# Attention into a routed two-layer MoE: a sum moved to the scalar engine, a copy moved ahead of an exponential, and the first loads and routing group regrouped

## The chip, the cores and the metric

The kernel runs on one core of one Trainium2 chip. The metric is the device time of one execution in microseconds (us), lower is better. Engines are named as in the profile: PE is TensorE (matmuls and transposes), PEld its weight loads, ACT is ScalarE, DVE is VectorE, POOL is GpSimd, SP is the sync engine, which here only issues DMAs. Each engine works through its own instructions in program order; order between engines is kept by semaphores.

## What is computed

The reference, cut to what matters. Attention is local: a row attends only within its chunk of 64.

```python
q_c, k_c, v_c = (a.reshape(8, 8, 9, 64, 64) for a in (q, k, v))      # B, H, chunks, 64, D
scores = np.matmul(q_c, k_c.transpose(0, 1, 2, 4, 3)) / np.sqrt(64)
scores = scores - np.max(scores, axis=-1, keepdims=True)
attn = np.exp(scores)
attn = attn / (np.sum(attn, axis=-1, keepdims=True) + 1e-09)
x = np.matmul(attn, v_c)  # then as 4608 tokens of 512
noisy = x @ w_gate + np.log1p(np.exp(x @ w_noise)) * noise            # 8 experts
# the two best experts of a token get weights top2_w = softmax of their two logits
out[token] = sum(top2_w[k] * (np.maximum(x[token] @ w1[e_k], 0) @ w2[e_k]) for k in (0, 1))
```

## The kernel before, in words

The 4608 tokens are 36 tiles of 128. The program has two stages.

**Attention and routing** is a software pipeline written out by hand: `attend(it)` (L672) is one turn, `it` from 0 to 39, and in it each engine gets work of several tiles. In turn `it` PE is given, in this order, the scores of tile it+1 (`scores`, L405, 16 recorded matmuls), probabilities times v of tile it-2 (`pv`, L433), on every fourth turn the router's matmul of the last four tiles (`gate_mm`, L463, line 465), the transposes of the probabilities of tile it-1 (`p_trans`, L423) and of the attention output of tile it-3 (`x_trans`, L450), and on the turn behind a gate turn the sums of the router's output (`gate_sum`, L475). DVE gets of tile `it` the row maxima (`soft_max`, L413) and their subtraction (`soft_sub`, L418), then of tile it-2 the norm in three steps: row sum plus 1e-9 (`norm_a`, L442), its reciprocal (`norm_b`, L445), and the product that evicts the attention output (`norm_c`, L448). ACT gets the exponential of tile `it` (`soft_exp`, L421), the copy of the transposed probabilities of tile it-1 out of PSUM (`p_copy`, L429), the copy of the transposed output of tile it-3 (`x_copy`, L459) and, in gate turns, one more copy (L469).

What matters for the steps below is what is single and what is double. Scores alternate between two PSUM banks. The result of `pv` has one place, banks 3 and 4 (`pvb`, L431): `norm_a` and `norm_c` read it, and `pv` of the next tile overwrites it. The transposed probabilities have one PSUM bank and two copies in SBUF, `mx` and `rc` have two buffers each.

**Routing** of a group of tiles (`route`, L480) is a generator of small DVE and ACT steps; a turn takes up to six DVE steps of it (`STEPS`, L673) behind `norm_c`. Groups are four tiles, the last eight (L109). When a group is routed, every tile of it is written twice to a table of slots in DRAM by an indirect DMA of POOL (`scatter`, L589; line 600). In front of each such write stands a tiny copy (L598) that makes POOL wait for the turn's `mx` or `rc`, so the writes are spread: one behind `mx`, one behind `rc`. POOL also does eight halves of the split of w1 (L89) in turns 12 to 26.

**The experts** follow: PE runs dense matmuls in three passes (`three`, L224, line 231) over tiles of tokens that are loaded back by expert. The first experts' blocks are loaded early, when the writes of a certain group are out (`EARLY`, L105).

Loads of q, k and v come per pair of tiles: `load_qk` (L321) and `load_v` (L328), on SP, into rings of three buffers. Only k of the first pair is issued by ACT (L341).

Of the kernel before, what the change touches and what calls it, by code (L numbers as in the profile page):

```python
# [8 lines left out]
FT = mybir.dt.float32  # L9
# [4 lines left out]
AF = mybir.ActivationFunctionType  # L14
OP = mybir.AluOpType
# [4 lines left out]
P = 128  # L20
NTOK = 4608
NT = NTOK // P
# [27 lines left out]
def kernel(ctx, tc, qT, kT, vh, wgn, noise, w1, w2, out, caps=CAPS):  # L50
    nc = tc.nc
    consts = ctx.enter_context(tc.tile_pool(name="consts", bufs=1))
# [49 lines left out]
    NJ = NLIST  # L102
    BN = max(sum(r for _, r in b) for bs in blocks for b in bs)
    LEAD = 7
    EARLY = {0: 3, 1: 6}  # L105


    NPE = nb
    groups = [(0, 4), (4, 4), (8, 4), (12, 4), (16, 4), (20, 4), (24, 4), (28, 8)]  # L109
    LAST = len(groups) - 1  # L110
    grp_of = {t: g for g, (t0, n) in enumerate(groups) for t in range(t0, t0 + n)}
    later_xg = []
# [5 lines left out]
    lwt = consts.tile([P, NJ, NE], FT, name="lwt")  # L118
    lid0 = {b: consts.tile([P, len(blocks[0][b])], I32, name=f"lid0{b}") for b in EARLY}
    lwt0 = {b: consts.tile([P, len(blocks[0][b])], FT, name=f"lwt0{b}") for b in EARLY}  # L120
    lim0 = {b: consts.tile([P, 1], FT, name=f"lim0{b}") for b in EARLY}
    meta0 = {b: consts.tile([P, len(blocks[0][b]), 3], FT, name=f"meta0{b}") for b in EARLY}
    XG, XH, HT, BX, BH, OB = {}, {}, {}, {}, {}, {}
# [9 lines left out]
    def rows_of(i, j):  # L133
        e = BL[i][0]
        k = j - blocks[0][i][0][0] if i in EARLY else 0
        return lid0[i][:, k:k + 1] if i in EARLY else lid[:, j, e:e + 1]

# [176 lines left out]
    loads = pk.enter_context(tc.tile_pool(name="loads", bufs=1))  # L314
    RING = 3
    KB = [loads.tile([P, 2, 2, 4, P], FT, name=f"kb{n}") for n in range(RING)]
    VB = [vs.tile([P, 2, 2, 2, 4, 65], FT, name=f"vb{n}") for n in range(RING)]
    QB = {}
    HALF = (slice(0, 64), slice(64, 128))

    def load_qk(j):  # L321
        if j < NT // 2:
            QB[j] = loads.tile([P, 2, 4, P], FT, name="qb", bufs=RING)
            for h in range(2):
                nc.sync.dma_start(QB[j][h::2], qT[HALF[h], 2 * j:2 * j + 2])
                nc.sync.dma_start(KB[j % RING][h::2, h], kT[HALF[h], 2 * j:2 * j + 2])
# [7 lines left out]
        nc.vector.memset(KB[0][:, :, a], 0.0)  # L334
    nc.gpsimd.memset(KB[1], 0.0)
    nc.vector.memset(VB[0], 0.0)
    QB[0] = loads.tile([P, 2, 4, P], FT, name="qb", bufs=RING)
    for a in range(2):
        for h in range(2):
            nc.sync.dma_start(QB[0][h::2, a], qT[HALF[h], a])  # L340
            nc.scalar.dma_start(KB[0][h::2, h, a], kT[HALF[h], a])  # L341
    nc.scalar.preload_act_table_set("natural_log_exp_and_others")
    load_v(0)
    jp = consts.tile([P, P], FT, name="jp")
# [4 lines left out]
    nc.vector.tensor_scalar(before, jp, 0.0, None, op0=OP.is_gt)  # L349
    ones = consts.tile([P, P], BF, name="ones")  # L350
    nc.vector.memset(ones, 1.0)
    spacer = consts.tile([1, 1], FT, name="spacer")
    e_row = consts.tile([P, NE], FT, name="e_row")
    nc.gpsimd.iota(e_row, pattern=[[1, NE]], base=0, channel_multiplier=0, allow_small_or_imprecise_dtypes=True)
# [24 lines left out]
    nc.gpsimd.memset(VB[1], 0.0)  # L379
    for t in (KB[2], VB[2]):  # L380
        nc.gpsimd.memset(t, 0.0)
    load_qk(1)
    load_v(1)
    wg = consts.tile([P, ND, 32], FT, name="wg")
    nc.sync.dma_start(wg, wgn)
# [9 lines left out]
    PR, PT, XS, XT, RC = {}, {}, {}, {}, {}  # L395
# [9 lines left out]
    def scores(t):  # L405
        for hp in range(4):
            for q in HALF:
                nc.tensor.matmul(PS[q, t % 2, hp * P:(hp + 1) * P], QB[t // 2][:, t % 2, hp, q],  # L408
                                 KB[t // 2 % RING][:, :, t % 2, hp, q], start=True, stop=True)
# [13 lines left out]
    def p_trans(t):  # L423
        for hp in range(4):
            nc.tensor.transpose(PS[:, 2, hp * P:(hp + 1) * P], PR[t][:, hp * P:(hp + 1) * P], ident)  # L425

    def p_copy(t):
        PT[t] = work.tile([P, 4, P], FT, name="pts", bufs=2)
        nc.scalar.activation(PT[t].rearrange("p a b -> p (a b)"), PS[:, 2, :], AF.Copy)  # L429

    pvb = PS[:, 3:5, 0:260].rearrange("p b (g n) -> p b g n", n=65)  # L431
# [7 lines left out]

    def norm_a(t):  # L440
        RC[t] = work.tile([P, 2, 4, 1], FT, name="rc", bufs=2)
        nc.vector.tensor_scalar(RC[t], pvb[:, :, :, 64:65], 1e-9, None, op0=OP.add)  # L442

    def norm_b(t):
        nc.vector.reciprocal(RC[t], RC[t])  # L445
# [34 lines left out]
    def route(g):  # L480
# [31 lines left out]
        m = gate.tile(n8, FT, name="gm")  # L512
        mi = gate.tile(n8, U32, name="gmi")
        for r in range(G):
            yield "dve"
            V.max(m[:, r], sp[:, r])
        for r in range(G):
            yield "dve"
            V.max_index(mi[:, r], m[:, r], sp[:, r])
        oh = gate.tile([P, 2, G, NE], FT, name="goh")  # L520
        for k in range(2):
# [67 lines left out]
    def scatter(n, gate=None):  # L589

        for _ in range(n):
            if not pending:
                return
            g, r, k = pending.pop(0)
            if gate is None:
                nc.gpsimd.memset(spacer, 0.0)
            else:
                nc.gpsimd.tensor_copy(spacer, gate)  # L598
            t0, G = groups[g]
            s = nc.gpsimd.indirect_dma_start(  # L600
                out=slots, out_offset=bass.IndirectOffsetOnAxis(ap=lii[:, k, t0 + r:t0 + r + 1], axis=0),
                in_=XS[(t0 + r) // 4][:, r % 4, 0:USED], in_offset=None)
            for o in scatters:
                tc.declare_no_dep(s.ins, o.ins, reason="every token has a slot of its own")
            for o in early_loads:
                tc.declare_no_dep(s.ins, o.ins, reason="slots of an early block are given before it is loaded")
            scatters.append(s)
            if (r, k) != (G - 1, 1):
                continue
            for i in EARLY:  # L610
                if g == EARLY[i]:
                    js = blocks[0][i][0][0]
                    m = len(blocks[0][i])
                    gather(i)
                    early_loads.append(nc.sync.dma_start(
                        meta0[i], by_slot[js * P:(js + m) * P, 0, CODE:USED].rearrange("(j p) c -> p j c", p=P)))
            if g == LAST:
                gather(len(EARLY))
# [18 lines left out]
    def step_route(phase, most=99):  # L637
        for r in list(routing):
            while r[1] == phase and most > 0:
                if phase == "dve":  # L640
                    most -= 1
                r[1] = next(r[0], None)
            if r[1] is None:
                routing.remove(r)
# [27 lines left out]
    def attend(it):  # L672
        STEPS = 6  # L673
        if it % 2:
            load_qk((it - 1) // 2 + 3)
        if it % 2 == 0 and it >= 4:
            load_v((it - 4) // 2 + 3)
        if it in (5, 7):
            for r in range(CLEAN + 64 * (it // 2 - 2), CLEAN + 64 * (it // 2 - 1), 16):
                nc.sync.dma_start(slots[r * NE:(r + 16) * NE, 0:USED], zero)  # L680
        if it == 7:
            nc.sync.dma_start(slots[(CLEAN + P) * NE:NLIST * P * NE, CODE:USED].rearrange("(p r) c -> p r c", p=P),
                              zero[:, 0:3 * (NLIST * P - CLEAN - P) // 16].rearrange("p (r c) -> p r c", c=3))
        if it in (9, 11, 13, 15):
            w_load(0, 1, (it - 9) // 2)
        if it == 32:
            zero_out(8)
        if it in (29, 31, 33, 35):
            w_load(0, 2, (it - 29) // 2)
        next_turn()  # L690
        if it == 0:
            scores(0)
        if it + 1 < NT:
            scores(it + 1)
        if 0 <= it - 2 < NT:
            pv(it - 2)
        gated = it - 4 >= 0 and (it - 4) % 4 == 3
        if gated:
            gate_mm((it - 4) // 4)
        if 0 <= it - 1 < NT:  # L700
            p_trans(it - 1)
        if 0 <= it - 3 < NT:
            x_trans(it - 3)
        if it - 5 >= 0 and (it - 5) % 4 == 3:
            gate_sum((it - 5) // 4)
            if grp_of[it - 5] != grp_of.get(it - 4):
                r = route(grp_of[it - 5])
                routing.append([r, next(r)])
        step_route("pe")
        if it < NT:  # L710
            mx = soft_max(it)
            soft_sub(it, mx)
            scatter(1, mx[0:1, 0, 0:1])
            soft_exp(it)
        if 0 <= it - 1 < NT:
            p_copy(it - 1)
        if 0 <= it - 3 < NT:
            x_copy(it - 3)
        if gated:
            gate_copy((it - 4) // 4)  # L720
        step_route("act")
        if 0 <= it - 2 < NT:
            norm_a(it - 2)
            norm_b(it - 2)
            scatter(1, RC[it - 2][0:1, 0, 0])
            norm_c(it - 2)
        step_route("dve", STEPS)
        if it > 32:
            zero_out(3)
        if it == NT + 2:  # L730
            scatter(2, XT[(it - 3) // 4][0:1, 0, (it - 3) % 4, 0:1])
        elif it == NT + 3:
            scatter(2, LS[(it - 4) // 4][0:1, 0, 0:1])
        if it in range(12, 28, 2):
            w_split(0, 1, *wq.pop(0), eng=nc.gpsimd)
# [241 lines left out]
```

## Time and profile before

| | us |
|---|---|
| median of three runs | 995.55 (994.05 to 995.59) |
| the profiled execution, its own time | 993.54 |
| its span, first to last instruction | 991.7 |
| busy: PE, DVE, ACT, POOL | 959.4, 463.9, 282.5, 225.8 |
| first scores matmul starts | 6.47 |
| first `pv` starts | 18.01 |
| `pv` of tile 34 starts | 143.55 |

The profile is one execution taken by the hardware profiler. In its lines `out<-in` gives the program's names, a shape is partitions x elements, `xN` counts instructions, and a bracket says how long the engine stood idle before the instruction and what ended that (`<-`). A fp32 matmul leaves two records, so `pv` of one tile shows as x16. The profiled time and the span differ by 1.8 us; the profiled execution lies 2.0 us below the median of the three runs.

### The profile page before, as it was taken

Reading aid. Unit: us, or ns where it says so; the run is one execution under the profiler, and the core shown is the slowest. Engines: PE = TensorE matmul, PEld = TensorE weight load, DVE = VectorE, ACT = ScalarE, POOL = GpSimd, SP = SyncE. Lnnn points to the kernel's source line nnn. Section 1 sums busy time; section 2 is a strip of 40 time slices with the busy share of each in tenths; the row PEclk is TensorE's granted clock in tenths of the full one; section 3 lists DMA queues with packets and bytes.
Section 4 is the critical chain, followed back from the end, with each engine's and each line's share of the span. In section 5 each row is a group of like instructions: output and inputs, shape, how many; then the busy total and the mean of one; then the engine's idle time right before and its main releaser. Section 6 shows DMA issues by size and latency. Waiting matters only on the chain.

```text
span 991.7 us, 16057 instructions
## 1 busy us (share of the span) xinstructions
PE 959.4 (97%) x5788; PEld 850.6 (86%) x5788; DVE 463.9 (47%) x1043; ACT 282.5 (28%) x595; POOL 225.8 (23%) x320
## 2 busy tenths in 40 slices
PE   6998988999999999999999999999999999999996
PEld 5886766898799888988998899889988998899885
DVE  6778774523445352544344434443344334433311
ACT  2565553222233221412231223132213221322100
POOL 3045556831100111121002101211111111111112
PEclk9999999999999999999999999999999999999999
DMA  8998899849611652166116622572264226402213
GB/s 300 317 368 285 293 376 395 268 143 149 180 33 33 154 136 37 33 142 149 35 28 136 159 48 28 112 178 44 32 154 133 44 32 154 112 12 32 33 22 44
DMA packets 97154, 132.92 MB, mean 134 GB/s; under 512 B 23440, under 2 KB 56592, under 8 KB 97072
## 3 DMA queue, kind: packets, MB, share of 16 engines
q1 hardware_dynamic: 80320, 93.02, 31.7%
q0 software_dynamic: 16432, 38.33, 19.3%
q8 instruction: 46, 0.75, 0.3%
q10 hardware_dynamic: 320, 0.52, 0.2%
q14 instruction: 36, 0.29, 0.1%
HBM read 81.69 MB, written 50.13 MB: 133 GB/s over the span
## 4 chain that ended last, share of the span: by engine, by line
PE 92%; DVE 4%; issue 2%; DMA 0%; POOL 0%; ACT 0%; another core or an unknown queue 0%; SPq 0%; DVEq 0%; POOLq 0%
PE PS L231 81%; PE PS L437 3%; PE PS L408 3%; PE PS L425 2%; PE PS L453 1%; PE PS L465 1%; PE PS L276 1%; DVE xs L448 1%; PE PS L478 1%; DMA kb<-in_kT 0%; POOL out L198 0%; DVE mx L413 0%; PE PS L214 0%; DVE pr L418 0%
## 5 line engine op out<-in xcount | busy, mean ns | idle before, releaser
L198 POOL DMA_INDIRECT out<-o,lid x77 | 119.9, 1557 | 662.0 <-DVE o L261 642.3
L231 PE MATMUL PS<-xh,w1h 128*128 128x384 f32 (+2 forms) x768 | 262.1, 341 | 4.8 <-issue 3.1
L231 PE MATMUL PS<-xl,w1h 128*128 128x384 f32 (+2 forms) x768 | 260.9, 340 | 0.2 <-DVE xl L222 0.2
L231 PE MATMUL PS<-xh,w1l 128*128 128x384 f32 (+2 forms) x768 | 260.9, 340 | 0.0
L250 ACT ACTIVATE hh<-PS 128x384 fp32r<-128x384 f32 (+2 forms) x192 | 95.2, 496 | 469.9 <-PE PS L231 421.3
L231 PE MATMUL PS<-w2h,hh 128*128 128x512 f32 x584 | 228.0, 390 | 0.0
L231 PE MATMUL PS<-w2h,hl 128*128 128x512 f32 x584 | 227.6, 390 | 0.0
L231 PE MATMUL PS<-w2l,hh 128*128 128x512 f32 x584 | 227.6, 390 | 0.0
L253 DVE SCALAR_TENSOR_TENSOR hl<-PS,hh 128x384 fp32r<-128x384 f32 (+2 forms) x192 | 108.6, 566 | 184.6 <-ACT hh L250 139.5
L261 DVE TENSOR_SCALAR o<-PS,lwt 128x512 f32<-128x512 f32 x77 | 57.7, 749 | 230.2 <-PE PS L231 222.9
L231 PEld LDWEIGHTS PS<-xh,w1h 128*128 128x128 f32 x768 | 144.5, 188 | 12.2 <-issue 8.2
L231 PEld LDWEIGHTS PS<-xl,w1h 128*128 128x128 f32 x768 | 144.6, 188 | 2.1 <-DVE xl L222 0.5
L231 PEld LDWEIGHTS PS<-xh,w1l 128*128 128x128 f32 x768 | 144.6, 188 | 1.0
L231 PEld LDWEIGHTS PS<-w2h,hl 128*128 128x128 f32 x584 | 109.2, 187 | 23.5
L231 PEld LDWEIGHTS PS<-w2h,hh 128*128 128x128 f32 x584 | 109.2, 187 | 22.5
L231 PEld LDWEIGHTS PS<-w2l,hh 128*128 128x128 f32 x584 | 109.2, 187 | 22.5
L600 POOL DMA_INDIRECT slots<-xs,lii x72 | 72.5, 1007 | 18.5 <-issue 17.9
L221 ACT ACTIVATE xh<-y 128x512 fp32r<-128x512 f32 x67 | 41.2, 614 | 92.6 <-DVE y L218 90.6
L222 DVE TENSOR_TENSOR xl<-y,xh 128x512 fp32r<-128x512 f32 x67 | 44.9, 671 | 48.2 <-ACT xh L221 45.4
L408 PE MATMUL PS<-kb,qb 128*64 128x128 f32 x576 | 43.2, 295 | 10.9 <-DMA kb<-in_kT 9.6
L408 PEld LDWEIGHTS PS<-kb,qb 128*64 128x64 f32 x576 | 34.0, 146 | 16.0 <-issue 13.0
L437 PE MATMUL PS<-vb,pts 128*64 128x130 f32 x576 | 40.2, 280 | 6.6 <-DVE gsm L543 1.7
(128 smaller groups left out, 701.2 us busy)
## 6 DMA issues: line engine op xcount, KB each, us to landing
st<-in_w SPq DMA_DIRECT2D x36, 512.0 KB
xg<-slots SPq DMA_DIRECT2D x252, 64.0 KB
st<-in_w SPq DMA_DIRECT2D x112, 128.0 KB
out<-zero SPq DMA_DIRECT2D x37, 256.0 KB
vb<-in_vh SPq DMA_DIRECT2D x36, 260.0 KB
qb<-in_qT SPq DMA_DIRECT2D x34, 256.0 KB
kb<-in_kT SPq DMA_DIRECT2D x34, 256.0 KB
xg<-slots SPq DMA_DIRECT2D x9, 256.0 KB
```

Of the source, the lines that this page charges most:

```text
L198: s = nc.gpsimd.indirect_dma_start(out=out, out_offset=bass.IndirectOffsetOnAxis(ap=rows_of(i, j)[0:r], axis=0), in_=o[0:r], in_offset=Non ...
L221: nc.scalar.activation(oh, src, AF.Copy)
L222: nc.vector.tensor_sub(ol, src, oh.bitcast(FT))
L231: nc.tensor.matmul(p, a, b, start=first and n == 0, stop=last and n == 2)
L250: nc.scalar.activation(hh[:, 0:n], p, AF.Relu)
L253: nc.vector.scalar_tensor_tensor(hl[:, 0:n], p, 0.0, hh[:, 0:n].bitcast(FT), op0=OP.max, op1=OP.subtract)
L261: nc.vector.tensor_scalar(o[0:r], p[0:r], w, None, op0=OP.mult)
L276: nc.tensor.matmul(p[q * r:q * r + r], HR[0][:, f, 0:r], staged[e, 2, f // 2][:, (f % 2) * DM:(f % 2) * DM + DM], start=n == 0, stop=n == ...
L408: nc.tensor.matmul(PS[q, t % 2, hp * P:(hp + 1) * P], QB[t // 2][:, t % 2, hp, q], KB[t // 2 % RING][:, :, t % 2, hp, q], start=True, stop ...
L425: nc.tensor.transpose(PS[:, 2, hp * P:(hp + 1) * P], PR[t][:, hp * P:(hp + 1) * P], ident)
L437: nc.tensor.matmul(PS[q, 3 + hp // 2, o:o + 130], PT[t][:, hp, q], VB[t // 2 % RING][:, :, t % 2, c, hp, :], start=True, stop=True)
L600: s = nc.gpsimd.indirect_dma_start(out=slots, out_offset=bass.IndirectOffsetOnAxis(ap=lii[:, k, t0 + r:t0 + r + 1], axis=0), in_=XS[(t0 + ...
```

## The change

Six edits, all in the attention stage.

1. q and k of the second pair of tiles are loaded right behind those of the first; k of it by ACT, ahead of the load of the activation table.
2. In turns 0 and 1 the PE order is other: scores of tiles 0 and 1, transposes of tile 0, scores of tile 2, then on as before.
3. On ACT, `p_copy(it-1)` stands ahead of `soft_exp(it)`; it stood behind it.
4. `norm_a` is an ACT activation (identity with a bias tile of 1e-9), placed behind `soft_exp(it)`, instead of a DVE operation.
5. The first routing group is tiles 0 to 7 in place of two groups of four, and `EARLY` is counted anew to name the same tiles. Two `max` or two `max_index` make one routing step, where one did.
6. In a turn two row writes stand behind `mx` in place of one, so a turn has up to three.

```diff
-    EARLY = {0: 3, 1: 6}
+    EARLY = {0: 2, 1: 5}
-    groups = [(0, 4), (4, 4), (8, 4), (12, 4), (16, 4), (20, 4), (24, 4), (28, 8)]
+    groups = [(0, 8), (8, 4), (12, 4), (16, 4), (20, 4), (24, 4), (28, 8)]
...
             nc.scalar.dma_start(KB[0][h::2, h, a], kT[HALF[h], a])
+    for h in range(2):
+        nc.sync.dma_start(QB[1][h::2], qT[HALF[h], 2:4])
+        nc.scalar.dma_start(KB[1][h::2, h], kT[HALF[h], 2:4])
     nc.scalar.preload_act_table_set("natural_log_exp_and_others")
     load_v(0)
...
-    load_qk(1)
     load_v(1)
...
     def norm_a(t):
         RC[t] = work.tile([P, 2, 4, 1], FT, name="rc", bufs=2)
-        nc.vector.tensor_scalar(RC[t], pvb[:, :, :, 64:65], 1e-9, None, op0=OP.add)
+        nc.scalar.activation(RC[t], pvb[:, :, :, 64:65], AF.Identity, bias=eps)
...
         for r in range(G):
-            yield "dve"
+            if r % 2 == 0:
+                yield "dve"
             V.max(m[:, r], sp[:, r])
...
         if it == 0:
             scores(0)
-        if it + 1 < NT:
+        if it <= 1:
+            p_trans(0) if it else scores(1)
+        if 0 < it < NT - 1:
             scores(it + 1)
...
+        if 0 <= it - 1 < NT:
+            p_copy(it - 1)
         if it < NT:
             mx = soft_max(it)
             soft_sub(it, mx)
-            scatter(1, mx[0:1, 0, 0:1])
+            scatter(2, mx[0:1, 0, 0:1])
             soft_exp(it)
-        if 0 <= it - 1 < NT:
-            p_copy(it - 1)
+        if 0 <= it - 2 < NT:
+            norm_a(it - 2)
         if 0 <= it - 3 < NT:
             x_copy(it - 3)
...
         if 0 <= it - 2 < NT:
-            norm_a(it - 2)
             norm_b(it - 2)
```

What ACT's program holds in turns 6 and 7, before: `pr` is the exponential, `pts` the copy of the transposed probabilities, `xt` the copy of the transposed output, `ls` the gate turn's extra copy (the numbers are those of the buffers).

```order
L421 ACTIVATE pr_416<-pr_416 128x512
L429 ACTIVATE pts_419<-PS_72 128x512
L459 ACTIVATE xt_299<-PS_72 128x4x128
L421 ACTIVATE pr_467<-pr_467 128x512
L429 ACTIVATE pts_470<-PS_72 128x512
L459 ACTIVATE xt_472<-PS_72 128x4x128
L469 ACTIVATE ls_474<-PS_72 128x512
```

And the same two turns now, where `rc` is the moved `norm_a`:

```order
L434 ACTIVATE pts_416<-PS_72 128x512
L426 ACTIVATE pr_420<-pr_420 128x512
L447 ACTIVATE rc_423<-PS_72,eps_143 128x8
L464 ACTIVATE xt_303<-PS_72 128x4x128
L434 ACTIVATE pts_467<-PS_72 128x512
L426 ACTIVATE pr_471<-pr_471 128x512
L447 ACTIVATE rc_474<-PS_72,eps_143 128x8
L464 ACTIVATE xt_476<-PS_72 128x4x128
L474 ACTIVATE ls_478<-PS_72 128x512
```

The copy and the exponential have changed places, and `rc` stands third, behind both.

On DVE, a plain turn and the head of the next before: maxima, subtraction, then the three steps of the norm.

```order
L413 TENSOR_REDUCE mx_331<-PS_72 128x8
L418 TENSOR_TENSOR pr_333<-PS_72,mx_331 128x4x2x64
L442 TENSOR_SCALAR rc_339<-PS_72 128x8
L445 RECIPROCAL rc_339<-rc_339 128x8
L448 TENSOR_TENSOR xs_261<-PS_72,rc_339 128x512
L413 TENSOR_REDUCE mx_376<-PS_72 128x8
```

Now:

```order
L418 TENSOR_REDUCE mx_335<-PS_72 128x8
L423 TENSOR_TENSOR pr_337<-PS_72,mx_335 128x4x2x64
L450 RECIPROCAL rc_340<-rc_340 128x8
L453 TENSOR_TENSOR xs_263<-PS_72,rc_340 128x512
L418 TENSOR_REDUCE mx_380<-PS_72 128x8
```

One instruction a turn is gone from DVE, and the reciprocal now reads what ACT has written.

At the start PE's program was this (`kb_108`, `kb_109` and `kb_110` are k of the first, second and third pair of tiles, `vb` is v):

```order
L408 MATMUL PS<-kb_108,qb 64x128 x16
L408 MATMUL PS<-kb_109,qb 64x128 x8
L425 MATMUL PS<-ident,pr 128x128 x4
L408 MATMUL PS<-kb_109,qb 64x128 x8
L437 MATMUL PS<-vb_111,pts 64x130 x8
```

and is now this:

```order
L413 MATMUL PS<-kb_108,qb 64x128 x16
L430 MATMUL PS<-ident,pr 128x128 x4
L413 MATMUL PS<-kb_109,qb 64x128 x16
L442 MATMUL PS<-vb_111,pts 64x130 x8
L430 MATMUL PS<-ident,pr 128x128 x4
```

The transposes of tile 0 stand ahead of the scores of tile 2.

More of the change, by code (lines that the diff above doesn't have):

```diff
@@ L336 @@
     nc.vector.memset(VB[0], 0.0)
-    QB[0] = loads.tile([P, 2, 4, P], FT, name="qb", bufs=RING)
+    for j in range(2):
+        QB[j] = loads.tile([P, 2, 4, P], FT, name="qb", bufs=RING)
     for a in range(2):
@@ L351 @@
     nc.vector.memset(ones, 1.0)
+    eps = consts.tile([P, 1], FT, name="eps")
+    nc.vector.memset(eps, 1e-9)
     spacer = consts.tile([1, 1], FT, name="spacer")
@@ L514, in route @@
         for r in range(G):
-            yield "dve"
+            if r % 2 == 0:
+                yield "dve"
             V.max(m[:, r], sp[:, r])
         for r in range(G):
-            yield "dve"
+            if r % 2 == 0:
+                yield "dve"
             V.max_index(mi[:, r], m[:, r], sp[:, r])
@@ L699, in attend @@
             gate_mm((it - 4) // 4)
-        if 0 <= it - 1 < NT:
+        if 0 < it - 1 < NT:
             p_trans(it - 1)
@@ L712, in attend @@
             soft_sub(it, mx)
-            scatter(1, mx[0:1, 0, 0:1])
+            scatter(2, mx[0:1, 0, 0:1])
             soft_exp(it)
-        if 0 <= it - 1 < NT:
-            p_copy(it - 1)
+        if 0 <= it - 2 < NT:
+            norm_a(it - 2)
         if 0 <= it - 3 < NT:
```

## The prediction

> **What bounds the kernel now.** I read the page, then the busy time by stretches, then the timeline of one turn.
>
> ```profile
> PE 959.4 (97%) x5788; PEld 850.6 (86%) x5788; DVE 463.9 (47%) x1043; ACT 282.5 (28%) x595; POOL 225.8 (23%) x320
> ```
> ```profile
> 18.00:36.00 18.00, 18.00 (x242) 15.11 (x240) 13.98 (x30) 8.83 (x16) 0.00 (x0) 1.00 0.95 338
> 112.00:128.00 16.00, 14.92 (x189) 12.18 (x186) 12.63 (x52) 8.49 (x20) 10.02 (x19) 1.00 0.91 309
> 148.00:174.00 26.00, 20.49 (x130) 17.40 (x130) 13.04 (x65) 8.71 (x21) 15.87 (x27) 0.93 1.04 395
> 174.00:230.00 56.00, 55.63 (x283) 48.79 (x284) 21.94 (x70) 11.04 (x22) 31.41 (x50) 1.00 0.68 188
> ```
>
> A stretch gives its length, then the busy time of PE, PEld, DVE, ACT and POOL, the granted clock, DMA share and GB/s. From 174 us on PE is busy 55.63 of 56: the experts are a block of matmuls, and whatever delays their start delays the end one for one. So the change is priced in the attention stage alone. There PE is full in plain turns (18.00 of 18.00) and nearly so with routing (14.92 of 16).
>
> One plain turn, from one `pv` to the next, in the timeline (start, duration):
>
> ```profile
> 26.59 1.06 PE L437 MATMUL PS<-vb,pts 128*64 128x130 f32 x16
> 27.58 0.65 PE L425 MATMUL PS<-ident,pr 128*128 128x128 f32 x4
> 27.70 0.17 DVE L442 TENSOR_SCALAR rc<-PS 128x8 f32<-128x8 f32 x1 [0.41 <-PE PS L437]
> 27.90 0.20 DVE L445 RECIPROCAL rc<-rc 128x8 f32<-128x8 f32 x1
> 28.14 0.69 DVE L448 TENSOR_TENSOR xs<-PS,rc 128x512 f32<-128x512 f32 x1
> 28.34 0.60 ACT L429 ACTIVATE pts<-PS 128x512 f32<-128x512 f32 x1 [0.38 <-PE PS L425]
> 28.83 0.59 ACT L459 ACTIVATE xt<-PS 128x512 f32<-128x512 f32 x1
> 29.53 1.06 PE L437 MATMUL PS<-vb,pts 128*64 128x130 f32 x16
> ```
>
> See that the norm starts 0.05 us after `pv` ends (26.59 + 1.06 = 27.65, then 27.70) and its eviction is over at 28.83, 0.70 before the next `pv` at 29.53 overwrites the banks. That slack is why PE sets the turn: 2.94 us.
>
> **The change: the norm moves onto a ring.** ACT runs in order. `norm_a(t)` now stands behind the exponential of tile t+2, that behind `p_copy(t+1)`, that waits for `p_trans(t+1)`, and that stands on PE behind `pv(t)`. And `pv(t+1)` may not start before `norm_c(t)` has read the banks. So from `pv` to `pv` runs one closed chain. Its links that the plain turn doesn't show, from waits of the same kind:
>
> ```profile
> 120.18 0.63 ACT L421 ACTIVATE pr<-pr 128x512 f32<-128x512 f32 x1 [1.34 <-DVE pr L418]
> 120.72 0.58 ACT L429 ACTIVATE pts<-PS 128x512 f32<-128x512 f32 x1
> 121.35 1.11 PE L437 MATMUL PS<-vb,pts 128*64 128x130 f32 x16
> 122.39 0.66 PE L425 MATMUL PS<-ident,pr 128*128 128x128 f32 x4
> ```
> ```profile
> 109.12 0.69 DVE L448 TENSOR_TENSOR xs<-PS,rc 128x512 f32<-128x512 f32 x1 [0.20 <-DVE rc L445]
> 109.95 1.11 PE L437 MATMUL PS<-vb,pts 128*64 128x130 f32 x16 [1.07 <-DVE xs L448]
> ```
> ```profile
> 149.12 0.60 ACT L221 ACTIVATE xh<-PS 128x512 fp32r<-128x512 f32 x1 [0.98 <-PE PS L214]
> 149.75 0.69 DVE L222 TENSOR_TENSOR xl<-PS,xh 128x512 fp32r<-128x512 f32 x1 [0.78 <-ACT xh L221]
> ```
> ```profile
> L496 ACT ACTIVATE gy<-PS 128x32 f32<-128x32 f32 x7 | 1.4, 200 | 1.7 <-PE PS L478 1.5 <-PE PS L535 0.2
> ```
>
> `pv` to `p_trans` 1.04 (121.35 to 122.39, a `pv` that had waited); `p_trans` to `p_copy` 0.76 (27.58 to 28.34); `p_copy` to the next on ACT 0.49 (28.34 to 28.83); exponential to the next 0.54 (120.18 to 120.72); `norm_a`, which no row shows on ACT, 0.21 (nearest: 200 ns for 32 columns out of PSUM, plus a little for the bias); ACT's end to DVE 0.03 (149.72 to 149.75); reciprocal to `norm_c` 0.24; `norm_c` 0.69; its end to `pv` 0.14 (109.81 to 109.95). Sum 4.14; I take **4.1 us a turn**, with 3.95 (`pv` not slowed by the wait, DVE to PE at nothing) and 4.3 as ends. PE's other work of the turn, `x_trans` and scores, fits beside it.
>
> The Trainium skill gives another price for `norm_a`: ScalarE: Activation LUTs, What ACT_TABLE_LOAD costs, has an activation whose bias is a pointer operand at about 280 ns plus 0.833 ns a column, so 0.29 by estimate. By that page the ring is 4.22 and the change 2.7 us dearer over the stage; no row here has this exact form, and the nearest is shorter.
>
> How many turns, and what they took:
>
> ```profile
> 18.01 1.28 PE L437 MATMUL PS<-vb,pts 128*64 128x130 f32 x16
> 143.55 1.11 PE L437 MATMUL PS<-vb,pts 128*64 128x130 f32 x16 [0.31 <-issue]
> L437 PE MATMUL PS<-vb,pts 128*64 128x130 f32 x544 | 37.8, 279 | 6.6 <-DVE gsm L543 1.7 <-ACT xt L459 1.2 <-ACT pr L421 1.2
> 33.45 1.06 PE L465 MATMUL PS<-xt,wg 128*32 128x512 f32 x8
> 34.45 0.66 PE L425 MATMUL PS<-ident,pr 128*128 128x128 f32 x4
> ```
>
> The group counts the window from 20 us: 544 / 16 = 34 `pv` behind the first, so 34 intervals took 143.55 - 18.01 = 125.5 us. All 34 go over the ring (the last exponential is in turn 35). In 8 of them the router's matmul lies between `pv` and `p_trans`: 1.00 more each (33.45 to 34.45). 34 x 4.1 + 8 x 1.0 = 147.4.
>
> **Routing steps** stand on DVE between `norm_c` and the next maxima:
>
> ```profile
> 71.10 0.18 DVE L503 SCALAR_TENSOR_TENSOR gu<-gu,gy 128x32 f32<-128x32 f32 x1
> 72.18 0.68 DVE L413 TENSOR_REDUCE mx<-PS 128x8 f32<-128x512 f32 x1
> ```
>
> Five opening steps take 1.08 (71.10 to 72.18). With steps R, maxima and subtraction (0.72 each: the 0.68 of the maxima taken for both, and a gap) end R + 1.34 after `pv`, while ACT gets to the exponential at 2.29 (1.04 + 0.76 + 0.49); so R up to 0.95 is hidden, and 1.95 in a gate turn. A full turn of six steps is some 1.2, and pairing two `max` a step fills more turns; about ten turns without a gate exceed by 0.25: +2.5 (0 to 5). What edits 4 and 5 take off DVE, 0.2 a turn and the steps of one group, is worth nothing while the ring ends later than DVE: 147.4 + 2.5 - 125.5 = **+24.4 us**. `p_copy` ahead of the exponential frees `pv` from a late subtraction, which shortens nothing while `pv` waits for `norm_c`.
>
> **The start.**
>
> ```profile
> 6.47 3.68 PE L408 MATMUL PS<-kb,qb 128*64 128x128 f32 x32 [6.47 <-DMA kb<-in_kT]
> 8.28 0.59 SPq L326 DMA_DIRECT2D kb<-in_kT  x1
> 9.93 0.63 ACT L421 ACTIVATE pr<-pr 128x512 f32<-128x512 f32 x1 [4.15 <-DVE pr L418]
> 13.29 1.98 PE L408 MATMUL PS<-kb,qb 128*64 128x128 f32 x16 [3.14 <-DMA kb<-in_kT]
> 15.20 1.12 PE L425 MATMUL PS<-ident,pr 128*128 128x128 f32 x4
> ```
>
> The scores of tile 2 wait 3.14 us for k, issued last at 8.28. Now it is issued ahead of v and should be there when the transposes of tile 0 are done: exponential over at 10.56, transposes 1.12, so about 11.7. Two tiles of scores at half of 3.68 each: `pv` at 15.4, or earlier as the clock rises, against 18.01: **-3.0** (-1 if the first k lands later for sharing, to -4).
>
> **Else.** POOL's writes come every 1.35 us:
>
> ```profile
> 89.33 1.01 POOL L600 DMA_INDIRECT slots<-xs,lii  x1 [0.16 <-issue]
> 90.68 0.99 POOL L600 DMA_INDIRECT slots<-xs,lii  x1 [0.16 <-issue]
> ```
>
> Three are 4.05, within a turn; only the first group's 16 beside three w1 halves run up to 2 us behind, which two buffers of `mx` and `rc` take up: 0 (0 to 2). DVE also waited for PE beyond what its program needs:
>
> ```profile
> DVE rc L442 <- remote: 3.7, 2, 2.1
> DVE rc L442 <- PE PS L453: 3.4, 2, 1.8
> ```
>
> The cause isn't shown. These 7.1 us lie in the 125.5; on the ring they may come on top: 0 to 7, I take +1.5. Behind the stage PE idles 5.5 of 26 us (148 to 174) while DMA is full (1.04); a longer stage leaves transfers less crowded: -1.5 (-4 to 0).
>
> Sum: 24.4 - 3.0 + 1.5 - 1.5 = +21.4. The profiled execution took 993.54, so 1014.9 on its scale; it lies 2.0 below the median of 995.55, on which I put the forecast: 1017, rounded down to **1016**.
>
> **Rivals.** *DVE is the bound and the ring is hidden* (faster). Where routing runs, DVE is busy 12.63 of 16, and DVE's waits for PE are few; if `norm_a` came in time, 34 x 0.2 = 6.8 from the moved sum (27.70 to 27.90), some 3 from a group's steps (five took 1.08; a group has about 20, and the double group's wider ones give part back) and 3.0 at the start: 995.5 - 12.8 = 983. It decides if the chain falls under the old mean of 125.5 / 34 = 3.69 a turn; `p_trans`, `p_copy` and exponential alone put `norm_a` at 2.83 of it, against the change. Chance 0.06.
>
> *The clock falls* (slower still). The ring leaves PE idle about 1 us in 4.
>
> ```profile
> 74.00:78.00 4.00, 2.26 (x28) 2.04 (x26) 2.65 (x9) 1.86 (x4) 2.39 (x4) 0.81 0.95 337
> 105.00:112.00 7.00, 5.44 (x67) 3.63 (x62) 4.52 (x16) 2.53 (x6) 4.84 (x9) 1.00 0.91 287
> ```
>
> With PE busy 2.26 of 4 the granted clock fell to 0.81; with 5.44 of 7 (78%) it stayed 1.00, and the ring is at 3.1 of 4.1 (76%). If a third of the 150 us ran at half clock, PE's two links (1.80) would double in 12 turns: +21.6, so 1038. Chance 0.07. The Trainium skill (TensorE: Matmul & The Clock Gate, Why this matters for your kernels) asks for gaps above about 3 us before the clock drops; by that rule this rival has no chance. The trace disagrees: at 74 the clock fell with 4.00 - 2.26 = 1.74 us idle in all.
>
> *The ring costs half* (slower, less): the waits for PE and the crowded stretch behind go, and routing turns, dearer than the mean of 3.69 before, lose little: 996 to 1004. Chance 0.08, a quarter of it within 0.2%.
>
> That the change does not do what it says is excluded by the order of instructions.
>
> **How the numbers follow.** Forecast 0.79. The range takes the ring at 3.95 (-5.1), no routing excess (-2.5), no recurring waits (-1.5) and the start and the stretch behind a little better (1004), and the ring at 4.3 (+6.8) with the waits at +7 (1028). A measurement here tells about 0.2%, 2 us. Faster 0.06, same 0.02, slower 0.92.
>
> **What would show it.** Right: plain turns of 4.1 us, with `norm_c` releasing `pv` in nearly every turn and the reciprocal waiting for ACT; first `pv` near 15. Wrong: plain turns still near 2.9, or `pv` released by PE's own order.

## The result and the profile after

| | before | after |
|---|---|---|
| median, us | 995.57 (994.05 to 997.12) | 1039.13 (1036.69 to 1040.5) |
| ratio, 95% interval | | 1.0435 (1.0409 to 1.0461) |
| the profiled execution, its own time and span | 993.54, 991.7 | 1036.69, 1034.7 |
| first `pv`, `pv` of tile 34 | 18.01, 143.55 | 14.27, 187.08 |

The change made the kernel slower, as forecast, but by 43.6 us, not 20.5: 1039.13 lies above the range of 1004 to 1028. The kernels below ran on several chips of the same kind; the kernel before took 981 to 982 us on two of them and 995 to 999 on the others, so every kernel is compared with the kernel before on its own chip, by ratio.

First the page's busy line and the stretches of after: the attention stage up to tile 18, the rest of it, and the experts.

```profile
PE 971.5 (94%) x5787; PEld 856.2 (83%) x5787; DVE 457.0 (44%) x993; ACT 284.9 (28%) x625; POOL 226.4 (22%) x320
```
```profile
14.20:94.70 80.50, 62.99 (x787) 50.07 (x782) 45.02 (x121) 37.44 (x90) 6.90 (x8) 1.00 0.78 260
94.70:187.00 92.30, 66.10 (x692) 51.63 (x692) 49.88 (x188) 36.35 (x96) 49.92 (x81) 0.87 0.83 295
...
217.00:300.00 83.00, 82.49 (x402) 72.52 (x403) 32.41 (x84) 19.83 (x39) 30.44 (x49) 0.98 0.66 157
```

PE is busy 62.99 of 80.50 us (78%) in the first half of the stage, where before it was full in plain turns. In the second half the granted clock is 0.87. Behind 217 us the experts run as before.

The start and the end of the stage, on PE:

```profile
14.27 1.07 PE L442 MATMUL PS<-vb,pts 128*64 128x130 f32 x16
...
17.95 1.09 PE L413 MATMUL PS<-kb,qb 128*64 128x128 f32 x16 [2.02 <-DMA kb<-in_kT]
...
187.08 1.21 PE L442 MATMUL PS<-vb,pts 128*64 128x130 f32 x10 [2.06 <-ACT ls L474]
```

The stage from `pv` of tile 0 to that of tile 34 takes 187.08 - 14.27 = 172.8 us, 47.3 more than the 125.5 before. The start gives back 3.7, and behind tile 34 the span has 1034.7 - 187.08 = 847.6 us left against 848.2. So the whole miss lies between tiles 0 and 34.

One plain turn of after, all engines, with DVE's and ACT's other rows left out:

```profile
63.00 1.11 PE L442 MATMUL PS<-vb,pts 128*64 128x130 f32 x16 [0.23 <-ACT gu L503]
...
64.03 0.66 PE L430 MATMUL PS<-ident,pr 128*128 128x128 f32 x4
...
64.73 0.60 ACT L434 ACTIVATE pts<-PS 128x512 f32<-128x512 f32 x1 [0.76 <-PE PS L430]
...
65.22 0.62 ACT L426 ACTIVATE pr<-pr 128x512 f32<-128x512 f32 x1
65.74 0.26 ACT L447 ACTIVATE rc<-PS,eps 128x8 f32<-128x8 f32 x1
...
66.03 0.20 DVE L450 RECIPROCAL rc<-rc 128x8 f32<-128x8 f32 x1 [1.86 <-ACT rc L447]
...
66.34 0.69 DVE L453 TENSOR_TENSOR xs<-PS,rc 128x512 f32<-128x512 f32 x1
...
67.14 1.11 PE L442 MATMUL PS<-vb,pts 128*64 128x130 f32 x16 [0.98 <-ACT xt L464]
```

This is the forecast ring, link by link: 1.03, 0.70, 0.49, 0.52, 0.29, 0.31, 0.69 and 0.11, in sum 4.14 us. PE's last wait is put down to ACT's `xt`, but `norm_c` ends at 67.03, 0.11 ahead of `pv`; that is the one it needs. Two links were longer than forecast, `norm_a` to reciprocal at 0.29 (0.24) and reciprocal to `norm_c` at 0.31 (0.24); the others were shorter by as much.

The second half is different. The turn from tile 18 to tile 19 takes 6.65 us instead of 4.2:

```profile
94.73 1.11 PE L442 MATMUL PS<-vb,pts 128*64 128x130 f32 x16 [1.04 <-issue]
...
95.76 0.99 POOL L607 DMA_INDIRECT slots<-xs,lii  x1 [0.16 <-issue]
...
95.77 0.66 PE L430 MATMUL PS<-ident,pr 128*128 128x128 f32 x4
...
97.32 0.98 POOL L607 DMA_INDIRECT slots<-xs,lii  x1 [0.40 <-issue]
...
98.64 0.98 POOL L607 DMA_INDIRECT slots<-xs,lii  x1 [0.16 <-issue]
...
98.93 0.60 ACT L434 ACTIVATE pts<-PS 128x512 f32<-128x512 f32 x1 [4.35 <-PE PS L483]
...
101.38 1.52 PE L442 MATMUL PS<-vb,pts 128*64 128x130 f32 x16 [2.69 <-ACT gu L503]
```

By PE's rows the transposes end at 95.77 + 0.66 = 96.43. ACT is free and waits for them, and its copy starts only at 98.93: 2.50 us late, where a plain turn has 0.04. I call this a late signal of PE. POOL's row writes stand back to back around it, five from 92.90 to 98.64. Three more such turns:

```profile
126.84 0.66 PE L430 MATMUL PS<-ident,pr 128*128 128x128 f32 x4
...
130.53 0.60 ACT L434 ACTIVATE pts<-PS 128x512 f32<-128x512 f32 x1 [5.29 <-remote]
...
145.13 0.66 PE L430 MATMUL PS<-ident,pr 128*128 128x128 f32 x4
...
149.43 0.60 ACT L434 ACTIVATE pts<-PS 128x512 f32<-128x512 f32 x1 [5.04 <-remote]
...
168.16 0.66 PE L430 MATMUL PS<-ident,pr 128*128 128x128 f32 x4
...
172.03 0.60 ACT L434 ACTIVATE pts<-PS 128x512 f32<-128x512 f32 x1 [4.61 <-remote]
```

"remote" means that no instruction in the trace ends where the wait does. The four are 2.50, 3.03, 3.64 and 3.21 us late, 12.4 in sum, and on the ring nothing hides them. Since the ends of matmuls are modelled, the rows don't tell whether PE's work or only its signal came late; the times of the semaphore updates, which the trace holds but no view prints, do. In the plain turn above PE's signals come 0.01 to 0.02 us behind the ends of its rows. In the last of the three turns here `pv` and the two sets of transposes end at 168.23, 168.82 and 169.26 by the rows, and their signals come at 171.94, 172.00 and 172.06, only 0.06 us apart, where the rows end 0.43 us and more apart. So the work was done, and its signals were held up.

POOL's rows up to 190 us hold just four runs of five writes with under 1.75 us from start to start, from 92.90, 123.89, 142.20 and 164.80 on, and each has one of the four late signals at its end. Beside the six runs of two or three ACT's copy never waits over 1 us for its signal; by the semaphore updates a signal of `pv` or of the scores is 1.1 to 1.9 us late behind each of the four runs of three, but the ring doesn't wait for that one. The length of a run isn't all: in the second trace of after (experiment 6) a run of six from 104.54 on brought no more than 1.1 us.

### The profile page after: what moved, and what is told of

It is laid out like the page before. It is cut to its first block, busy times and chain, and to the rows that moved or that the text cites. A ratio compares the mean times of both kernels' runs of the same rounds, so it can differ in the third digit from the quotient of the medians.

```text
span 1034.7 us, 16013 instructions
## 1 busy us (share of the span) xinstructions
PE 971.5 (94%) x5787; PEld 856.2 (83%) x5787; DVE 457.0 (44%) x993; ACT 284.9 (28%) x625; POOL 226.4 (22%) x320
## 4 chain that ended last, share of the span: by engine, by line
PE 83%; DMA 6%; ACT 3%; DVE 2%; issue 2%; POOL 1%; SPq 1%; another core or an unknown queue 0%; DVEq 0%; ACTq 0%; POOLq 0%
PE PS L231 77%; PE PS L442 2%; DMA kb<-in_kT 1%; PE PS L430 1%; DMA vb<-in_vh 1%; DMA out<-zero 1%; ACT pr L426 1%; PE PS L276 1%; DMA st<-in_w 1%; ACT pts L434 1%; DMA slots<-xs,lii 1%; PE PS L470 1%; DVE xs L453 1%; DMA slots<-zero 1%
## 5 line engine op out<-in xcount | busy, mean ns | idle before, releaser
L442 PE MATMUL PS<-vb,pts 128*64 128x130 f32 x576 | 44.5, 299 | 39.6 <-ACT ls L474 8.4
L442 PEld LDWEIGHTS PS<-vb,pts 128*64 128x64 f32 x576 | 35.9, 147 | 47.0 <-ACT ls L474 9.9
```

The source lines that it names most:

```text
L442: nc.tensor.matmul(PS[q, 3 + hp // 2, o:o + 130], PT[t][:, hp, q], VB[t // 2 % RING][:, :, t % 2, c, hp, :], start=True, stop=True)
```

## The experiments

Two theories at first. **R**: the ring alone lays late signals open, whatever the writes do. **W**: the third row write (edit 6) makes them. A third, **X**, came up with the first traces: the output rows. The rows of four tiles share one of five buffers, which comes free when their eight writes have landed, and the group of eight (edit 5) starts the writes later. A fourth, **C**, came up with the chips: the late signals belong to the chip and come with any writes.

**1. The ring alone.** The kernel before with edits 3 and 4:

```diff
+        if 0 <= it - 1 < NT:
+            p_copy(it - 1)
...
             soft_exp(it)
-        if 0 <= it - 1 < NT:
-            p_copy(it - 1)
+        if 0 <= it - 2 < NT:
+            norm_a(it - 2)
```

> The kernel before with edits 3 and 4 alone (copy ahead of the exponential, norm_a on ACT behind it): the ring, without the new start, the group of eight and the third row write. Theory W (the late turns are long because PE's results are signalled 2.5 to 3.6 us late where five or more row writes follow each other 1.3 us apart): with two writes a turn the runs of writes are short, plain turns of 4.2 us from first to last, 1017 to 1025. Theory R (the ring alone lays the late signals open, however the writes are grouped, and the clock falls for it): as after less the start's gain, 1038 to 1046.

Measured: 1017.11 us against 982.04, ratio 1.0358 (1.0327 to 1.0388). The turns are 4.1 to 4.3 us from first to last, with no late signal. The time is what W expected, but the kernel before was 13 us faster on this chip than on the first, so the ratio fitted neither and the question had to be put again on other chips.

**2. After without the ring.** `norm_a` back on DVE, everything else as in after:

```diff
-        nc.scalar.activation(RC[t], pvb[:, :, :, 64:65], AF.Identity, bias=eps)
+        nc.vector.tensor_scalar(RC[t], pvb[:, :, :, 64:65], 1e-9, None, op0=OP.add)
...
-        if 0 <= it - 2 < NT:
-            norm_a(it - 2)
...
         if 0 <= it - 2 < NT:
+            norm_a(it - 2)
             norm_b(it - 2)
```

> The kernel after with norm_a back on DVE at its old place; everything else stays. Both theories: no ring, plain turns of 2.9 to 3.2 us. Theory W: the third write still bunches the writes, late signals of 2 us and more stay and cost 3 to 8 us, 994 to 1002. Theory R: only the start's gain of 3.7 us and what DVE saves are left, 985 to 993.

Measured: 995.37 against 982.04, ratio 1.0128 (1.0096 to 1.0161). So edits 5 and 6 cost something without the ring too, as W said, but on this chip not by late signals (none): `norm_c` of tile 20 waited 5.3 us for row writes, the clue to X.

**3. After with two writes a turn.**

```diff
-            scatter(2, mx[0:1, 0, 0:1])
+            scatter(1, mx[0:1, 0, 0:1])
```

> The kernel after with one row write behind the maxima instead of two, so two a turn. Theory W: the four late signals of 2.5 to 3.6 us go or fall under 1.5 us, the clock keeps to 1.00 up to tile 30, 1015 to 1026. Theory R: they stay, 1035 to 1043.

Measured: 1045.11 against 982.04, ratio 1.0657 (1.0621 to 1.0694): neither. Taking the third write out of after made it worse (after itself was at 1.0435 on the first chip). DVE in the turn of tile 20:

```profile
111.79 0.69 DVE L453 TENSOR_TENSOR xs<-PS,rc 128x512 f32<-128x512 f32 x1 [4.96 <-DMA slots<-xs,lii]
```

`norm_c` writes into the buffer of tiles 0 to 3 and waits until the last of its eight writes has landed. Two writes a turn are eight in four turns, just what four tiles bring, so a late start is never made up: such a wait came at tiles 20, 24, 28 and 32 (turns of 8.2 to 9.2 us). So with edit 5 in place the third write also has its use: with it `norm_c` hardly waits (experiments 5 to 8).

**4. The new start alone.** Edits 1 and 2 on the kernel before.

```diff
+    for h in range(2):
+        nc.sync.dma_start(QB[1][h::2], qT[HALF[h], 2:4])
+        nc.scalar.dma_start(KB[1][h::2, h], kT[HALF[h], 2:4])
...
+        if it <= 1:
+            p_trans(0) if it else scores(1)
```

> The kernel before with edits 1 and 2 alone (second pair's q and k loaded first, order of turns 0 and 1). If the start's gain reaches the end: first pv near 14.3 instead of 18.0 and 992 (-3.7). Rival: the later turns wait for their loads or for the slots and give it back: 994 to 997.

Measured: ratio 1.000 (0.9985 to 1.0015). PE at the start of this kernel, and the third `pv` of the kernel before (on the first chip):

```profile
13.85 1.05 PE L440 MATMUL PS<-vb,pts 128*64 128x130 f32 x16
...
18.13 1.09 PE L411 MATMUL PS<-kb,qb 128*64 128x128 f32 x16 [2.64 <-DMA kb<-in_kT]
...
23.61 1.05 PE L440 MATMUL PS<-vb,pts 128*64 128x130 f32 x16
```
```profile
23.66 1.06 PE L437 MATMUL PS<-vb,pts 128*64 128x130 f32 x16
```

The first `pv` comes 4 us earlier, then the scores of a later tile wait for the next k, and by the third `pv` the gain is gone (23.61 against 23.66). The load was not moved out of the way, only the wait for it moved. With the ring part of the gain stays (experiment 9).

**5 to 8. Which chip, which edit.** On another chip, with the kernel before run for its profile, the kernel after again, after with edit 5 undone, and before with edit 5 alone:

```diff
-    groups = [(0, 8), (8, 4), (12, 4), (16, 4), (20, 4), (24, 4), (28, 8)]
+    groups = [(0, 4), (4, 4), (8, 4), (12, 4), (16, 4), (20, 4), (24, 4), (28, 8)]
```

(with `EARLY` and the routing steps as before; edit 5 alone is the same lines the other way round, on the kernel before)

> The kernel before, unchanged, for its profile on the chip of this call. If this chip is like the one of the first experiments: about 982, plain turns of 2.9 us and none of the late signals of PE that stood between 66 and 145 us; if like the first chip, 994 to 996.

> The kernel after, unchanged, beside its parts on the same chip. Theory X (the ring, plus a ring of buffers: the output rows of four tiles hold a buffer of five until their eight writes have landed; the group of eight starts the writes some four turns later, so from tile 20 on norm_c waits for them): ratio to before 1.045 to 1.06, with waits of norm_c for row writes of 3 to 6 us at every fourth tile. Theory R (the ring, plus late signals of PE as on the first chip): ratio 1.036 or less if this chip shows no late signals.

> The kernel after with edit 5 undone: groups of four, one max a step, the early blocks as before. Theory X: no wait of norm_c for row writes, plain turns of 4.2 us to the end, ratio 1.030 to 1.038, that of the ring alone. Theory R: as the kernel after beside it, within 0.5%.

> The kernel before with edit 5 alone: the first group of eight, steps in pairs, early blocks renumbered. Theory X: two writes a turn of 2.9 us start some four turns later and never catch up, so norm_c waits for them from tile 20 on, once per four tiles: 5 to 20 us slower, ratio 1.005 to 1.02. Theory R: 0 to 3 us, ratio 0.997 to 1.003.

Measured: before 995.32, with late signals; after 1.0459 (1.0409 to 1.0510), with late signals of 2.5 to 4.1 us in the same four turns as in its first trace; after with groups of four 1.0450 (1.0404 to 1.0496); before with the group of eight 1.0283 (1.0234 to 1.0332). So X falls for after, though the ratio is the one it forecast: undoing edit 5 changes nothing there, and `norm_c` hardly waits for row writes. By itself, though, with two writes a turn, edit 5 costs 27 us, more than X expected. The waits of `norm_c` in the first trace of after (14 to 190 us), with ACT's waits that end at nothing, and in before with edit 5 (20 to 170 us); the columns are total, times, longest:

```profile
ACT pts L434 <- remote: 14.9, 3, 5.3
...
DVE xs L453 <- DMA slots<-xs,lii: 0.8, 3, 0.3
```
```profile
DVE xs L448 <- DMA slots<-xs,lii: 26.3, 4, 7.2
```

**9. Ring and start, without edits 5 and 6**, on one of the 981 us chips:

> The kernel after with edits 5 and 6 undone: groups of four and two row writes a turn, so the ring and the new start alone. Theory W (three writes a turn make PE's results late where five follow each other): plain turns of 4.2 us throughout, no late signal over 1 us, ratio 1.031 to 1.038. Theory C (the late signals belong to the chip and come with any writes): on a chip like the first, late signals of 2 to 4 us stay and the ratio is 1.041 to 1.050; on a chip without them 1.031 to 1.038.

Measured: ratio 1.0314 (1.0290 to 1.0339), no late signal, as both theories allow on such a chip. It is 0.4% under the ring alone (1.0358 on another chip of that kind), but the intervals overlap, so the ratios don't show that the start's gain is kept. The traces do in part: the first `pv` comes at 13.80 against 17.61 with the ring alone, the third at 23.66 against 25.95, so 2.3 of the 3.8 us are left by then.

**10. The third write alone**, edit 6 on the kernel before, same chip.

> The kernel before with edit 6 alone, three row writes a turn. My recorded step has it at nothing (0 to 2 us): ratio 0.998 to 1.003. Theory W: late signals of 2 to 4 us where five writes follow each other, half of it hidden by the slack of plain turns: ratio 1.005 to 1.015. Theory C: as the kernel before, 0.998 to 1.003.

Measured: ratio 1.0061 (1.0042 to 1.0080). The ratio is the one W forecast, but not for W's reason. ACT's copy starts over 1 us behind the transposes twice, by 2.2 and 1.2 us, and both times ACT was held by its exponential, which waited for DVE's subtraction:

```profile
72.15 0.66 PE L425 MATMUL PS<-ident,pr 128*128 128x128 f32 x4
...
74.44 0.63 ACT L421 ACTIVATE pr<-pr 128x512 f32<-128x512 f32 x1 [3.45 <-DVE pr L418]
74.97 0.58 ACT L429 ACTIVATE pts<-PS 128x512 f32<-128x512 f32 x1
```

By the semaphore updates no signal of PE is over 1 us late in this trace, although POOL's writes stand in runs of up to eight there. My step had the third write at nothing (0 to 2); here it cost 7.4 us, and by what wasn't traced.

**11. The same work, another place.** Edits 3 and 4, but `norm_a` at the head of ACT's turn:

```diff
+        if 0 <= it - 2 < NT:
+            norm_a(it - 2)
         if 0 <= it - 1 < NT:
             p_copy(it - 1)
...
             soft_exp(it)
-        if 0 <= it - 2 < NT:
-            norm_a(it - 2)
```

> The kernel before with edits 3 and 4, but norm_a at the head of ACT's turn, ahead of p_copy, in place of behind the exponential. The work is that of the ring kernel, only the place differs. Ring theory: from pv by norm_a, reciprocal and norm_c back to pv is 1.1 + 0.3 + 0.3 + 0.7 + 0.1 = 2.5 us, under the 2.94 of PE, so plain turns of 2.9 us and a ratio of 0.99 to 1.005. Rival (ACT's longer form or its load is the cost, wherever it stands): 1.02 to 1.035.

Measured: ratio 1.0014 (1.0000 to 1.0029). A stretch of 78 us (PE's busy time first), and one turn:

```profile
18.00:96.00 78.00, 78.00 (x1029) 66.48 (x1030) 62.58 (x206) 54.42 (x134) 27.81 (x40) 1.00 0.99 359
```
```profile
85.82 1.06 PE L439 MATMUL PS<-vb,pts 128*64 128x130 f32 x16
...
86.98 0.27 ACT L444 ACTIVATE rc<-PS,eps 128x8 f32<-128x8 f32 x1 [0.30 <-issue]
...
87.28 0.20 DVE L447 RECIPROCAL rc<-rc 128x8 f32<-128x8 f32 x1
...
87.58 0.69 DVE L450 TENSOR_TENSOR xs<-PS,rc 128x512 f32<-128x512 f32 x1
```

`norm_c` is over at 88.27, 2.45 us after `pv` began, and PE is full again. So the 32 to 35 us of the ring on such chips are the place of `norm_a`, not its work.

**12. The copy ahead alone**, edit 3 on the kernel before, same chip.

> The kernel before with edit 3 alone, the copy of the probabilities ahead of the exponential. My recorded step prices it at nothing as long as pv waits for norm_c; without the ring the copy no longer waits for a late subtraction: ratio 0.990 to 1.001. Rival: the exponential comes 0.6 us later and with it the next transposes, 1.003 to 1.01.

Measured: ratio 1.0007 (0.9993 to 1.0020), so nothing. (The prediction had priced this edit at nothing with the ring; this is without it.)

**13 to 16. All on one chip of the 996 us kind.** The kernel after, experiment 9, experiment 10 and experiment 2 once more:

> The kernel after, unchanged, beside the three that follow on one chip. On a chip with late signals of PE: ratio 1.043 to 1.048. On a chip without: theory W+C (the third write and the chip's late signals make the late turns) 1.033 to 1.042; theory X (the five buffers of output rows, held longer by the group of eight) the waits of norm_c stay whatever the chip, 1.045 to 1.055.

> The kernel after with edits 5 and 6 undone (ring and new start alone), unchanged from the run before. Without late signals 1.031 again. With them: theory W (it takes three writes a turn) 1.031 to 1.036, no late signal over 1 us; theory C (any writes do on such a chip) 1.040 to 1.048.

> The kernel before with edit 6 alone, unchanged from the run before. Without late signals on this chip 1.006 again; with them, theory W 1.01 to 1.02, theory C 0.998 to 1.006.

> The kernel after with norm_a back on DVE, unchanged from the run before, for what the ring alone is worth in after on one chip. If ring and buffers are two costs that add: after minus this is 30 to 35 us on a chip without late signals. If the ring hides the wait for buffers (longer turns give the writes more time): 18 to 28 us.

| on this chip (before 998.60) | us | ratio | writes a turn | late signals over 1 us, sum |
|---|---|---|---|---|
| after | 1045.38 | 1.0469 (1.0423 to 1.0514) | 3 in 4.2 us | 4, 13.6 us |
| ring and start | 1023.67 | 1.0235 (1.0183 to 1.0288) | 2 in 4.2 us | none |
| before + third write | 1014.38 | 1.0160 (1.0108 to 1.0211) | 3 in 2.9 us | 7, 19.4 us |
| after, `norm_a` on DVE | 1011.27 | 1.0148 (1.0096 to 1.0201) | 3 in 2.9 us | 6, 18.4 us |
| (before, experiment 5, another chip of the kind) | | | 2 in 2.9 us | 4, 6.9 us |

A late signal is counted here where ACT stood idle and its `p_copy` started over 1 us after PE's row of the transposes ends; where the copy only stood behind a late exponential it isn't counted. On this kind of chip this settles R and C against W: the ring with two writes a turn has no late signal on the very chip on which after has four, and by the semaphore updates none of PE's other signals is over 1 us late there either, up to 187 us. What counts is the run, not the third write as such: the kernel before, with two writes in shorter turns, has four late signals, one behind each run of three. The ratio of ring and start is still below all three forecasts (1.031 and more). A likely reason is that the kernel before has late signals of its own on this kind of chip, which the ring loses; no run shows that apart. The first two rows differ by 21.7 us, edits 5 and 6; edit 5, undone by itself, was worth nothing (experiment 7, on another chip of the kind). Ring and start: writes, one turn, `pv` of tiles 0, 18 and 34, and the stretch from 96 us on.

```profile
14.88 1.05 PE L442 MATMUL PS<-vb,pts 128*64 128x130 f32 x16
...
95.09 1.11 PE L442 MATMUL PS<-vb,pts 128*64 128x130 f32 x16 [0.80 <-ACT ls L474]
...
137.32 0.98 POOL L605 DMA_INDIRECT slots<-xs,lii  x1 [0.51 <-issue]
...
139.21 0.98 POOL L605 DMA_INDIRECT slots<-xs,lii  x1 [0.51 <-issue]
...
140.32 0.65 PE L430 MATMUL PS<-ident,pr 128*128 128x128 f32 x4
...
141.01 0.60 ACT L434 ACTIVATE pts<-PS 128x512 f32<-128x512 f32 x1 [2.38 <-PE PS L430]
...
141.55 0.98 POOL L605 DMA_INDIRECT slots<-xs,lii  x1 [0.51 <-issue]
...
166.68 1.17 PE L442 MATMUL PS<-vb,pts 128*64 128x130 f32 x16 [2.06 <-ACT ls L474]
```
```profile
96.00:166.50 70.50, 55.52 (x680) 44.37 (x676) 46.06 (x176) 36.27 (x96) 38.87 (x63) 1.00 0.87 293
```

The writes stand mostly 1.9 to 2.3 us apart (in the whole stage never more than two within 1.75 us of each other), ACT follows the transposes by 0.04 us, and the clock is 1.00 to the end of the stage. Against that the kernel before with the third write, where five writes stand 1.3 us apart from 110.07 us on:

```profile
111.56 0.66 PE L425 MATMUL PS<-ident,pr 128*128 128x128 f32 x4
...
114.05 0.98 POOL L600 DMA_INDIRECT slots<-xs,lii  x1 [0.16 <-issue]
...
115.36 0.98 POOL L600 DMA_INDIRECT slots<-xs,lii  x1 [0.16 <-issue]
...
115.83 0.17 DVE L442 TENSOR_SCALAR rc<-PS 128x8 f32<-128x8 f32 x1 [3.59 <-remote]
...
117.31 0.60 ACT L429 ACTIVATE pts<-PS 128x512 f32<-128x512 f32 x1 [4.40 <-remote]
```

Transposes over at 112.22, the copy at 117.31: 5.09 us late. After and experiment 16 differ by 34.1 us, what the ring is worth with edits 5 and 6 beside it; ring and start alone came to 25.1. So the two costs more than add: 25.1 and the 12.7 by which experiment 16 is slower than before make 37.8 us, and after is 46.8 slower. (The 34.1 lie in the range that the expectation gave for a chip without late signals; this chip has them.)

**17. What is left.** After with edits 5 and 6 undone and `norm_a` at the head of ACT's turn:

> The kernel after with edits 5 and 6 undone and norm_a at the head of ACT's turn: what is left of the change once its two costs are out (new start, copy ahead, norm_a off DVE). If the parts that measured 0.0, 0.1 and 0.1 per cent alone stay nothing together: ratio 0.998 to 1.003. If the start's 3 us and DVE's 0.2 us a turn come through once both are there: 0.990 to 0.997, a version that beats both kernels.

Measured: ratio 0.9998 (0.9983 to 1.0013). No part of the change showed a gain, and no run points to a version that beats the kernel before.

## Why the prediction was wrong

- **The ring** (plain turns of 4.1, 147.4 us for 34 intervals, and 2.5 for routing): right. Plain turns mostly took 4.14 to 4.24, gated ones 5.2. In ring and start on the 996 us kind of chip the 34 intervals are 166.68 - 14.88 = 151.8 us; the forecast with its waits was 151.4 (the terms for routing and waits, 4.0 us of it, were not measured apart). The kernel came out 25.1 us slower, against 21.4 in my sum. The Trainium skill (ScalarE: Activation LUTs, What ACT_TABLE_LOAD costs) gave about 0.29 us for `norm_a` where I took 0.21; its row has 0.26, so that price was the nearer one. From its start to the reciprocal it is 0.29, where my two links made 0.24.
- **The start**, -3.0: right for the first `pv` of after (14.27 against 18.01, -3.7), but that is not a gain at the end. Beside the ring some 2.3 us of it are left by the third `pv` (experiment 9); in experiment 13 hardly any were (25.88 against 25.95 with the ring alone); alone it is worth nothing.
- **The third write: this step failed.** I wrote "Three are 4.05, within a turn" and priced it at 0 (0 to 2). That asked only whether POOL has the time. It has, and that is the trouble: its writes then follow each other without a gap, and in such runs PE's signals reached ACT and DVE 2.5 to 3.6 us late in after. Edits 5 and 6 measured 21.7 us together where the ring is, edit 5 undone by itself changed nothing, and the third write cost 15.8 us without the ring on that chip. On a faster chip it cost 7.4 us without any late signal, so late signals are not all of its price.
- **The waits of unknown cause**, +1.5 (0 to 7): the same thing under another name. The kernel before has them where its own writes stand close: four over 1 us, each at the end of a run of three. I took them as a fixed amount that the change doesn't touch; two writes in a longer turn remove them, three bring back 12.4 us.
- **The clock** (a rival, 1038): its time was near, its mechanism was not. The ring, busy 55.52 of 70.50 us, kept the clock at 1.00. In after it fell behind the late turns. By estimate from its row, a mean of 0.87 over 92.3 us is 0.26 of it, 24 us, at half speed; a turn there is 4.2 + 1.8 = 6.0 us, so four turns lose 1.8 each, 7.2 us. With the 12.4 us of late signals that is 19.6 of the 20.7 us by which tiles 18 to 34 took longer than in ring and start (92.3 against 166.68 - 95.09 = 71.6).
- **Behind the stage**, -1.5: measured -0.6, within its bounds. **DVE's savings** at nothing and **the copy ahead** at nothing: right as far as experiments 11 and 12 show, in which nothing was gained either (ratios 1.0014 and 1.0007).
- **The range** missed because both terms that depend on POOL's writes were bounded from the kernel before, which makes two writes a turn. The rivals "DVE is the bound" and "the ring costs half" fell with the 4.2 us turns.

What stays open: what holds PE's signals up. That runs of writes and late signals come together on the 995 to 999 us chips is shown; that the writes hold the signals up is the likely reading, but no run separates their bytes from their number or from POOL's work on them. Why the 981 to 982 us chips show no late signal even with three writes a turn wasn't tried.

## What to carry to other kernels

When a step moves to another engine, draw the closed chain from one use of a single buffer to the next, in each engine's program order; its sum is the turn, and here it was right to 2%. The same step at the head of ACT's turn cost next to nothing. And a transfer that fits its engine's time is not free for that: ask whether it still leaves gaps, and what waits of unknown cause in the trace stand beside such runs; whoever packs them denser should price those waits as growing with it. And before a late start is put down to a late signal, see whether the engine that starts late was idle.

## What the runs showed of the hardware

- **Row writes back to back and PE's signals.** On the 996 us kind of chip, runs of five and more of POOL's indirect writes, mostly 1.3 us apart, brought waits for PE that ended up to 5.1 us late; one run of six brought only 1.1. Runs of three, as in the kernel before, gave 1.1 to 2.3 us. With never more than two in a row, on the same chip, none was over 1 us late in 36 turns. What is late is the signal: in after three came 0.06 us apart, up to 3.7 us behind rows that end 0.43 us and more apart.
- **Chips differ in it.** The kernel before took 981 to 982 us on two chips and 995 to 999 on the others. On the second kind it has four late signals, of 6.9 to 7.0 us in sum; in none of the eight traces on the first kind is a signal of PE over 1 us late in the attention stage, not even beside runs of six to eight writes (experiments 2 and 10).
- **The clock.** PE idle about 1 us in every 4.2 for 150 us left the granted clock at 1.00. It fell behind longer gaps in PE's rows: 2.7 us in after (98.68 to 101.38, the clock from 101.9), 2.6 us in experiment 11 (113.26 to 115.84, the clock from 115.8), and two of 2.1 us in experiment 14 (159.37 to 161.48 and 164.61 to 166.68, the clock from 167.6). The Trainium skill (TensorE: Matmul & The Clock Gate, Why this matters for your kernels) warns of gaps above about 3 us; by these rows the clock fell behind shorter ones too, as the prediction had read from 74 to 78 us of before. Experiment 11 ran on a chip without late signals. No run here measures the limit.
